# Retention ahead of two expert layers: one PE tiling for three steps, decayed keys on three engines, three load buffers

## The chip, the cores and the metric

The program runs on one core of a Trainium2 chip. The metric is the time of one execution on the device in microseconds (us). Before the change it was 1789.78 us, the median of three runs (1785.21, 1789.78 and 1790.85). Differences under about 0.3% can't be told from no change.

## The reference, cut to what matters

Retention over 4 batches, 8 heads, 576 positions and 64 features gives 2304 rows of 512 values; they pass a mixture of 8 experts whose gate is normalised eight times over rows and columns, and then a two-layer net. Inputs and output are float32.

```python
scores = scale * np.matmul(q, k.transpose(0, 1, 3, 2))
Dmat = np.where(rel >= 0, gamma[:, None, None] ** rel[None, :, :], 0.0)
ret = scores * Dmat[None, :, :, :]
attn_out = np.matmul(ret, v)
# x = attn_out as (2304, 512)
for e in range(8):
    h = np.maximum(x @ w1[e], 0.0)
    out += P[:, e:e + 1] * (h @ w2[e])
# moe2
h = x @ w_in; g = np.maximum(0.01 * h, h); y = g @ w_out
```

## The kernel before

The expert layers take some 1700 us and the change touches none of their code. It lies in the first part, the retention, which is done in 18 chunks (n = 0 to 17; N = 18) of 128 rows. The two halves of the batch alternate, so that even and odd n are two independent streams; each pair works through a sequence of 576 positions in four chunks of 128, and the last two chunks hold the 64-row ends of the sequences. A chunk whose place in its sequence is 0 (n = 0, 1, 8, 9) has no state from earlier chunks.

Each chunk has two loads of 512 KB: `qk` (queries and keys, features on the partitions) and `vk` (values and keys, positions on the partitions). Both come from SyncE's queue (SP), each kind into four rotating buffers. A load into a buffer waits until all readers of the chunk that was there are done. SP also carries the decay tables `gq_t` (256 KB), two halves of the first expert's weights `raw` (1 MB each, at n = 3 and n = 11), the stores of finished operand tiles `x` (256 KB a chunk, from n = 9 on), rows of scales (`s_dram`, `inv`) and the loads of operand tiles back into `xring` (384 KB each).

For chunk n TensorE (PE) does, in this order in pass n of the loop:

- `emit_qk(n + 1)`, L695: scores of the next chunk into two PSUM banks `sc`; VectorE (DVE) multiplies them by the decay mask into `w` (L697)
- `emit_state(n)`, L725: decayed queries `qd` times the running state, into the two banks `xo`
- `emit_du(n)`, L754: decayed keys times values, added to the state's bank `du`; ScalarE (ACT) copies it to `state` (L756)
- `emit_scale(n - 1)`, L764: column sums of the magnitudes `ab` of the chunk before, by a product with ones; DVE makes a power of two of them (L767) and scales both `xo` banks with it into an operand tile (L770)
- `emit_intra(n)`, L735: `w` times values, added to `xo`; ACT takes the magnitudes into `ab` (L739)

The queries are decayed on GpSimd (POOL) two chunks ahead (`decay_q`, L669, 128x512, two buffers `qd`). The keys are decayed one chunk ahead (`decay_k`, L678): three heads (128x192) on DVE and five (128x320) on POOL. A scaled tile is split in a high and a low half: ACT casts (L829), DVE subtracts (L831).

Beside this the first expert's weights are prepared. Their small tasks wait in a list `pre`, and `step()`, called four times a chunk, emits at most one that is ready; `PACE` is the least number of steps between two tasks of the same engine (POOL "G" and DVE "D"). The instructions of an engine run strictly in the order in which they were emitted.

At the end two 512-column products `mark` (L952) start the banks `s2` of the expert layers, and then the first expert product (hA, L1053) begins. The last chunk's `emit_scale` and what hangs on it stand in `drain`, from which `tick` takes one entry when its counter `wait[0]` has run out.

Of the kernel before, what the change touches and what calls it, by code (L numbers as in the profile page):

```python
# [22 lines left out]
NP = H // 2  # L23
# [108 lines left out]
def retention_moe_ffn_kernel(ctx: ExitStack, tc: tile.TileContext, qk, vk, wg, wm, wf,  # L132
# [475 lines left out]
    with ExitStack() as actx:  # L608
# [23 lines left out]
        def load_qk(n):  # L632
            if n < N:
                qks[n] = ain.tile([P, 2, 512], F32, tag="qk", name=f"qk{n}", bufs=4)
                nc.sync.dma_start(qks[n].rearrange("p a x -> p (a x)"), qk[n])

        def load_vk(n):
            if n < N:
                vks[n] = ain.tile([P, 2, 512], F32, tag="vk", name=f"vk{n}", bufs=4)
                nc.sync.dma_start(vks[n].rearrange("p a x -> p (a x)"), vk[n])  # L640
# [9 lines left out]
        for i in range(36):  # L650
            nc.tensor.matmul(wu[:, :P], ones_b, ones_b, start=True, stop=True)
# [3 lines left out]
        nc.vector.memset(low_e, -896.0 * 2.0 ** 23)  # L655
        load_qk(0)
# [5 lines left out]
        load_qk(2)  # L662
        nc.scalar.activation(warm_a, tiny, AF.Abs)
        wt, qds, xo_t, halves, rows_, abs_t = {}, {}, {}, {}, {}, {}
# [6 lines left out]
        def decay_k(n):  # L671

            if n < N - 2:
                kd = vks[n][:, 1].rearrange("p (h d) -> p h d", h=H)
                c = chunk_of(n)[1]
                for e, h, k in ((nc.vector, 0, 3 if n > 1 else H), (nc.gpsimd, 3, H if n > 1 else 3)):
                    if k > h:
                        e.tensor_tensor(kd[:, h:k], kd[:, h:k],  # L678
                                        gk_t[:, c, h:k].unsqueeze(2).to_broadcast([P, k - h, D]), op=ALU.mult)
# [5 lines left out]
        def emit_qk(n):  # L685
# [5 lines left out]
            wt[n] = awk.tile([P, 2, NP, C], F32, tag="w", name=f"w{n}")  # L691
            if n < N - 2:
                for m in range(NP):
# [5 lines left out]
            for pb in range(2):  # L699
                nc.gpsimd.memset(wt[n][rows(pb), :, :, rows(1 - pb)], 0.0)  # L700
            for m in range(NP):
                for pb in range(2):
                    for j in range(2):
                        nc.tensor.matmul(sc[j][rows(pb), m, rows(pb)], kv[rows(j), m, rows(pb)],
                                         qv[rows(j), m, rows(pb)], start=True, stop=True)
            for j in range(2):
# [51 lines left out]
        def emit_scale(n):  # L758
# [4 lines left out]
            for m in range(NP):  # L763
                nc.tensor.matmul(l1, ones_b, ab[:, m], start=(m == 0), stop=m == NP - 1, skip_group_check=True)  # L764
# [88 lines left out]
        PACE = {"G": 2, "D": 3}  # L853
        emit_qk(0)
        for n in range(N):
            load_qk(n + 3)
            load_vk(n + 2)
            keeps(n)
# [13 lines left out]
            def step():  # L872
                wait[0] += 1
                order.t = 0.86 * wait[0]
                if n < 4:
                    return
# [17 lines left out]
                if n >= N - 4:  # L894
                    try_loads()

            decay_q(n + 2)
            if n:
                emit_qk(n + 1)
            step()  # L900
# [5 lines left out]
            if n >= 1:  # L906
                emit_scale(n - 1)
            step()
# [4 lines left out]
            decay_k(n + 1)  # L913
# [9 lines left out]
            step()  # L923
            if n % 2 and 2 * NT_S <= (n - 2) // 2 < 8:
# [13 lines left out]
        wait[0] = 0  # L938
# [10 lines left out]
    s2 = [bank(f"du{i}", f"s2_{i}") for i in range(2)]  # L949
    s1 = [bank(f"x{i}", f"s1{t}") for i, t in enumerate("ab")]  # L950
    def mark(t):
        nc.tensor.matmul(t.rearrange("p (a i) -> p a i", a=4), ones_b,  # L952
                         ones_b.unsqueeze(1).to_broadcast([P, 4, P]), start=True, stop=True)

    for t in s2:
        mark(t)
# [653 lines left out]
```

## Time and profile before

| | |
|---|---|
| median of three runs | 1789.78 us |
| the profiled execution | 1784.0 us |
| its span | 1781.9 us |
| PE busy | 1750.5 us, 98% of the span |
| DVE, ACT, POOL busy | 1500.0, 1262.0 and 821.7 us |
| granted TensorE clock, mean | 0.998 |
| first product of the expert layers | starts at 76.95 us |

The profiled execution is one of its own; the 2.1 us between it and its span lie before the first and after the last instruction. The chain of waits says which work ended last, step by step; "idle before" in a row is the engine's idle time ahead of the instruction, with what ended it. PEld are the weight loads of PE, which run ahead of its products.

### The profile page before, as it was taken

Reading aid. Unit: us, or ns where it says so; the run is one execution under the profiler, and the core shown is the slowest. Engines: PE = TensorE matmul, PEld = TensorE weight load, DVE = VectorE, ACT = ScalarE, POOL = GpSimd, SP = SyncE. Lnnn points to the kernel's source line nnn. Section 1 sums busy time; section 2 is a strip of 40 time slices with the busy share of each in tenths; the row PEclk is TensorE's granted clock in tenths of the full one; section 3 lists DMA queues with packets and bytes.
Section 4 is the critical chain, followed back from the end, with each engine's and each line's share of the span. In section 5 each row is a group of like instructions: output and inputs, shape, how many; then the busy total and the mean of one; then the engine's idle time right before and its main releaser. Section 6 shows DMA issues by size and latency. Waiting matters only on the chain.

```text
span 1781.9 us, 36082 instructions
## 1 busy us (share of the span) xinstructions
PE 1750.5 (98%) x13782; PEld 1275.9 (72%) x13782; DVE 1500.0 (84%) x2660; ACT 1262.0 (71%) x2757; POOL 821.7 (46%) x794
## 2 busy tenths in 40 slices
PE   8999999999999999999999999999999989999998
PEld 7755677777777777777777777777776556777776
DVE  7877899988888888888888888988776887788876
ACT  4667677777777777777777777777675667877653
POOL 3676262635445272625354453636124973444600
PEclk9999999999999999999999999999999999999999
DMA  9854353534544435445354454453443444435232
GB/s 352 312 199 157 116 171 109 191 120 163 158 139 158 159 123 172 144 144 187 113 178 136 146 170 145 138 166 106 136 154 101 160 157 145 144 98 164 81 121 84
DMA packets 205474, 272.48 MB, mean 153 GB/s; under 512 B 13922, under 2 KB 173044, under 8 KB 200180
## 3 DMA queue, kind: packets, MB, share of 16 engines
q1 hardware_dynamic: 205300, 270.17, 46.4%
q8 instruction: 108, 1.77, 0.4%
q14 instruction: 66, 0.54, 0.1%
HBM read 239.31 MB, written 30.81 MB: 152 GB/s over the span
## 4 chain that ended last, share of the span: by engine, by line
PE 92%; DVE 3%; POOL 2%; DMA 1%; issue 1%; ACT 1%; SPq 0%; DVEq 0%; POOLq 0%; ACTq 0%
PE s L1257 17%; PE hA L1084 12%; PE hB L1084 12%; PE hE L1084 12%; PE s1a L1257 12%; PE s1b L1257 11%; PE hD L1084 6%; PE s L1299 2%; PE s1b L1299 1%; PE s1a L1299 1%; PE hE L1053 1%; PE hA L1053 1%; PE hD L1053 1%; PE hB L1053 1%; PE sc L695 1%
## 5 line engine op out<-in xcount | busy, mean ns | idle before, releaser
L1084 PEld LDWEIGHTS <-w 128*128 128x128 f16 x4788 | 468.9, 98 | 237.7 <-issue 3.5
L1257 PEld LDWEIGHTS <-hs 128*128 128x128 f16 x3888 | 380.6, 98 | 88.0 <-ACT hs L1165 4.9
L1257 PEld LDWEIGHTS <-hp 128*128 128x128 f16 x2916 | 285.3, 98 | 82.7 <-issue 3.6
L275 POOL TENSOR_TENSOR w<-raw,w 128x384 f16<-128x384 f32 x148 | 163.7, 1121 | 311.8 <-ACT w L265 311.2
L1270 DVE SCALAR_TENSOR_TENSOR y<-s,fac,y 128x256 f32<-128x256 f32 (+1 forms) x322 | 197.6, 614 | 95.7 <-PE s L1257 80.4
L282 POOL TENSOR_TENSOR raw<-raw 128x256 f32<-128x256 f32 x296 | 268.8, 908 | 19.8
L1257 PE MATMUL s<-w,hs 128*128 128x256 f16 x1932 | 264.3, 273 | 0.2 <-ACT s L1275 0.2
L1084 PE MATMUL hB<-xring,w 128*128 128x384 f16 x1368 | 260.0, 326 | 1.9 <-ACT hB L1094 1.9
L1084 PE MATMUL hA<-xring,w 128*128 128x384 f16 x1368 | 261.1, 327 | 0.0
L1084 PE MATMUL hE<-xring,w 128*128 128x384 f16 x1368 | 260.7, 327 | 0.0
L1175 DVE TENSOR_TENSOR hs<-fs,hs 128x768 f16<-128x768 f32 (+1 forms) x228 | 238.2, 1050 | 12.1 <-ACT hs L1165 11.4
L300 POOL TENSOR_TENSOR w<-raw,w 128x512 f16<-128x512 f32 x148 | 195.6, 1337 | 96.0 <-ACT w L294 95.9
L459 POOL TENSOR_TENSOR f<-f,e 128x256 f32<-128x256 f32 x64 | 53.4, 835 | 365.2 <-DVE e L451 321.2
L1165 ACT ACTIVATE hs<-fs 128x768 f16<-128x768 f32 (+1 forms) x228 | 187.4, 823 | 47.9 <-DVE fs L1200 40.2
L1165 ACT ACTIVATE hp<-fp 128x384 f16<-128x384 f32 x240 | 160.5, 677 | 12.7 <-DVE fp L1123 11.9
L1270 DVE SCALAR_TENSOR_TENSOR y<-s1a,fac,y 128x256 f32<-128x256 f32 (+1 forms) x161 | 98.8, 614 | 51.2 <-ACT s L1275 26.4
L1257 PE MATMUL s1a<-w,hs 128*128 128x256 f16 x972 | 133.6, 273 | 5.5 <-ACT hs L1165 4.4
L1257 PE MATMUL s1a<-w,hp 128*128 128x256 f16 x972 | 132.8, 273 | 1.6 <-DVE y L1270 1.0
L1257 PE MATMUL s1b<-w,hs 128*128 128x256 f16 x960 | 131.5, 273 | 2.1 <-DVE hs L1175 1.7
L1270 DVE SCALAR_TENSOR_TENSOR y<-s1b,fac,y 128x256 f32<-128x256 f32 (+1 forms) x161 | 98.8, 613 | 40.2 <-ACT s L1275 18.1
L1257 PE MATMUL s1b<-w,hp 128*128 128x256 f16 x960 | 131.1, 273 | 1.5 <-DVE y L1270 1.5
L1257 PE MATMUL s<-w,hp 128*128 128x256 f16 x966 | 131.8, 273 | 0.0
(207 smaller groups left out, 2748.2 us busy)
## 6 DMA issues: line engine op xcount, KB each, us to landing
xring<-x SPq DMA_DIRECT2D x407, 384.0 KB, 3.8
raw<-in_wm SPq DMA_DIRECT2D x32, 1024.0 KB, 6.3
r<-in_wf SPq DMA_DIRECT2D x64, 256.0 KB, 3.0
x<-xst SPq DMA_DIRECT2D x51, 256.0 KB, 2.0
qk<-in_qk SPq DMA_DIRECT2D x18, 512.0 KB, 5.1
vk<-in_vk SPq DMA_DIRECT2D x18, 512.0 KB, 8.2
wf_s<-f SPq DMA_DIRECT2D x32, 256.0 KB, 2.6
raw<-wf_s SPq DMA_DIRECT2D x8, 1024.0 KB, 5.8
```

Source lines behind the costliest of these rows:

```text
L275: nc.gpsimd.tensor_tensor(v[0], v[1], v[2], op=ALU.subtract)
L282: nc.gpsimd.tensor_tensor(o, x, y_, op=ALU.subtract)
L300: nc.gpsimd.tensor_tensor(lo, r, hi, op=ALU.subtract)
L459: nc.gpsimd.tensor_tensor(dst, dst, cur["tx"].bitcast(F32), op=ALU.mult)
L695: nc.tensor.matmul(sc[j][:, m], kv[rows(j), m], qv[rows(j), m], start=True, stop=True)
L1053: nc.tensor.matmul(bank, w[:, a, wi, k, :], x[:, :, c, k, :], start=q == k == i == 0, stop=q == k == 1 and i == 2, skip_group_check=True)
L1084: nc.tensor.matmul(bank, w[:, a, wi, k, :], x[:, :, b, k, :], start=r in (1, 5) and k == q == 0, stop=k == 1 and q == 2, skip_group_check= ...
L1165: nc.scalar.activation(hid[k][:, 0, a:b], src[:, a:b], AF.Relu if moe and relu else AF.Copy)
L1175: nc.vector.tensor_tensor(t[:, 1, a:b], src[:, a:b], t[:, 0, a:b], op=ALU.subtract)
L1257: nc.tensor.matmul(out_, t[:, a, i, ts], w[:, b, wi, 0, :], start=start and k == 0, stop=k == 5, skip_group_check=True)
L1270: nc.vector.scalar_tensor_tensor(out_, bank, f, out_, op0=ALU.mult, op1=ALU.add)
L1299: nc.tensor.matmul(bank, t[:, a, i, ts], w[:, b], start=l == g == q == 0, stop=l == g == 1 and q == 2, skip_group_check=True)
```

## The change

The row and column tiling of the product for magnitudes becomes that of the two products on either side of it (two products of 64 output rows in place of one of 128). Keys are decayed on three engines (one head on DVE, six on POOL, one on ACT) at the head of a pass instead of late in it, ahead of `decay_q` and `emit_qk`. POOL's weight tasks stand at least 5 steps apart instead of 2. There are three buffers of each kind, `qk` is loaded two chunks ahead instead of three, and the last `vk` one pass earlier. The zeroing for the two end chunks and their masks are moved, one `mark` goes to the start and one into pass 16, and the drain starts four ticks later.

```diff
 def load_qk(n):
-        qks[n] = ain.tile([P, 2, 512], F32, tag="qk", name=f"qk{n}", bufs=4)
+        qks[n] = ain.tile([P, 2, 512], F32, tag="qk", name=f"qk{n}", bufs=3)
 def load_vk(n):
-    if n < N:
-        vks[n] = ain.tile([P, 2, 512], F32, tag="vk", name=f"vk{n}", bufs=4)
+    if n < N and n not in vks:
+        vks[n] = ain.tile([P, 2, 512], F32, tag="vk", name=f"vk{n}", bufs=3)
...
-        for i in range(36):
+        for i in range(33):
             nc.tensor.matmul(wu[:, :P], ones_b, ones_b, start=True, stop=True)
...
+        s2 = [None, bank("du1", "s2_1")]
+        mark(s2[1])
         load_qk(0)
...
         load_qk(1)
         load_vk(1)
-        load_qk(2)
...
-                for e, h, k in ((nc.vector, 0, 3 if n > 1 else H), (nc.gpsimd, 3, H if n > 1 else 3)):
-                    if k > h:
-                        e.tensor_tensor(kd[:, h:k], kd[:, h:k],
-                                        gk_t[:, c, h:k].unsqueeze(2).to_broadcast([P, k - h, D]), op=ALU.mult)
+                for e, h, k in ((nc.vector, 0, 1), (nc.gpsimd, 1, H - 1)) if n > 1 else ((nc.vector, 0, H),):
+                    e.tensor_tensor(kd[:, h:k], kd[:, h:k],
+                                    gk_t[:, c, h:k].unsqueeze(2).to_broadcast([P, k - h, D]), op=ALU.mult)
+                for i in range(k, H):
+                    nc.scalar.activation(kd[:, i], kd[:, i], AF.Copy, scale=gk_t[:, c, i:i + 1])
...
             for m in range(NP):
-                nc.tensor.matmul(l1, ones_b, ab[:, m], start=(m == 0), stop=m == NP - 1, skip_group_check=True)
+                for i in range(2):
+                    nc.tensor.matmul(l1[rows(i)], ones_b[:, :64], ab[:, m], start=(m == 0), stop=m == NP - 1,
+                                     skip_group_check=True)
...
-        PACE = {"G": 2, "D": 3}
+        PACE = {"G": 5, "D": 3}
         emit_qk(0)
         for n in range(N):
-            load_qk(n + 3)
+            load_qk(n + 2)
             load_vk(n + 2)
+            if n == N - 4:
+                load_vk(N - 1)
...
+            clear(n + 1)
+            if n:
+                decay_k(n + 1)
             decay_q(n + 2)
             if n:
                 emit_qk(n + 1)
+            if n == N - 3:
+                last_masks(N - 2)
             step()
             emit_state(n)
...
             if n >= 1:
                 emit_scale(n - 1)
+            if n == N - 2:
+                last_masks(N - 1)
             step()
             if n:
                 emit_intra(n)
             else:
                 emit_qk(1)
-            decay_k(n + 1)
+                decay_k(1)
...
+            if n == N - 2:
+                s2[0] = bank("du0", "s2_0")
+                mark(s2[0])
...
-        wait[0] = 0
+        wait[0] = 4
```

`clear` zeroes on POOL the parts of an end chunk's `w` that stay zero, and `last_masks` holds the four mask products of an end chunk; both were inside `emit_qk` before.

On SP, near the end of the retention, the loads of the last two chunks (qk16, vk16, qk17, vk17) stand among stores `x0_1<-xf` and loads `xring` like this before:

```order
L635 DMA qk17_1120<-in_qk 128x1024
L640 DMA vk16_1122<-in_vk 128x1024
L499 DMA x0_1_96<-xf11_1051 128x1024
L776 DMA s_dram_90<-s12_1099 1x128
L524 DMA xring_101<-x0_1_96 128x3x512 x2
L640 DMA vk17_1186<-in_vk 128x1024
```

and like this now:

```order
L635 DMA qk16_1181<-in_qk 128x1024
L640 DMA vk16_1183<-in_vk 128x1024
L640 DMA vk17_1185<-in_vk 128x1024
L499 DMA x0_1_96<-xf11_1107 128x1024
L795 DMA s_dram_90<-s12_1162 1x128
L524 DMA xring_101<-x0_1_96 128x3x512 x2
L635 DMA qk17_1260<-in_qk 128x1024
```

The last `vk` moved ahead of the two `xring` loads, and the last `qk` moved behind them. vk17 takes the buffer of vk14, so it waits for chunk 14's values to have been read, and all that follows on SP waits with it.

On DVE, around chunk 9 (w9 is its mask product, vk8 and vk9 the decayed keys), the rows before are:

```order
L767 TENSOR_SCALAR s6_697<-xo6_0_606 128x128
L770 SCALAR_TENSOR_TENSOR y3_114<-xo6_0_606,s6_697 128x256
L770 SCALAR_TENSOR_TENSOR y3_114<-xo6_1_607,s6_697 128x256
L678 TENSOR_TENSOR vk8_590<-vk8_590,gk_t_136 128x192
L831 TENSOR_TENSOR xring_101<-first1_491,xring_101 128x2x256
L226 TENSOR_REDUCE mt0_715<-mg0_669 32x1
L227 STREAM_TRANSPOSE t32_84<-mt0_715 32x32
L697 TENSOR_TENSOR w9_729<-sc9_0_727,dt_t_135 128x512
```

and now:

```order
L786 TENSOR_SCALAR s6_731<-xo6_0_631 128x128
L789 SCALAR_TENSOR_TENSOR y3_114<-xo6_0_631,s6_731 128x256
L789 SCALAR_TENSOR_TENSOR y3_114<-xo6_1_632,s6_731 128x256
L850 TENSOR_TENSOR xring_101<-first1_510,xring_101 128x2x256
L226 TENSOR_REDUCE mt0_747<-mg0_699 32x1
L227 STREAM_TRANSPOSE t32_84<-mt0_747 32x32
L683 TENSOR_TENSOR vk9_680<-vk9_680,gk_t_136 128x64
L704 TENSOR_TENSOR w9_764<-sc9_0_762,dt_t_135 128x512
```

The decay of vk9, a third as wide, stands directly ahead of chunk 9's masks, where that of vk8 stood behind the scaling of chunk 6.

On POOL, chunks 11 to 14, with the weight tasks L360 between the decays, before:

```order
L678 TENSOR_TENSOR vk11_787<-vk11_787,gk_t_136 128x320
L360 TENSOR_TENSOR w0_0_0_895<-raw0_0_382,w0_0_0_895 128x4x128
L669 TENSOR_TENSOR qd13_923<-qk13_847,gq_t_137 128x512
L360 TENSOR_TENSOR w0_0_0_895<-raw0_0_382,w0_0_0_895 128x4x128
L678 TENSOR_TENSOR vk12_849<-vk12_849,gk_t_136 128x320
L360 TENSOR_TENSOR w0_0_1_938<-raw0_0_382,w0_0_1_938 128x4x128
L669 TENSOR_TENSOR qd14_993<-qk14_915,gq_t_137 128x512
L360 TENSOR_TENSOR w0_0_1_938<-raw0_0_382,w0_0_1_938 128x4x128
L678 TENSOR_TENSOR vk13_917<-vk13_917,gk_t_136 128x320
```

and now:

```order
L675 TENSOR_TENSOR qd12_898<-qk12_889,gq_t_137 128x512
L360 TENSOR_TENSOR w0_0_0_944<-raw0_0_389,w0_0_0_944 128x4x128
L683 TENSOR_TENSOR vk12_891<-vk12_891,gk_t_136 128x384
L675 TENSOR_TENSOR qd13_973<-qk13_962,gq_t_137 128x512
L683 TENSOR_TENSOR vk13_964<-vk13_964,gk_t_136 128x384
L675 TENSOR_TENSOR qd14_1046<-qk14_1036,gq_t_137 128x512
L360 TENSOR_TENSOR w0_0_0_944<-raw0_0_389,w0_0_0_944 128x4x128
L683 TENSOR_TENSOR vk14_1038<-vk14_1038,gk_t_136 128x384
```

Four weight tasks that stood within two chunks now stand one in every one or two chunks, and the decay of the keys comes ahead of that of the queries in each pass.

## Rows read from the trace of the kernel before

**Rows 1.** The page's first line.

```profile
span 1781.9 us, 36082 instructions
```

**Rows 2.** Chain of waits, from 55 to 78 us: start us, us, what.

```profile
66.99 0.65 SPq L524
...
69.01 5.91 DMA vk<-in_vk
```

**Rows 3.** Timeline of PE, one chunk: start us, us, engine, line, operation, count.

```profile
35.18 1.16 PE L695 MATMUL sc<-qk 64*128 64x128 f32 x16
36.27 0.67 PE L725 MATMUL xo<-qd,state 64*64 64x128 f32 x16
36.87 0.69 PE L754 MATMUL du<-vk 128*64 128x64 f32 x16
37.48 0.40 PE L764 MATMUL xo<-ab,ones_b 128*128 128x128 bf16 x4
37.81 1.09 PE L735 MATMUL xo<-w,vk 128*64 128x128 f32 x16
38.83 0.60 PE L695 MATMUL sc<-qk 64*128 64x128 f32 x6
```

**Rows 4.** Timeline of PEld at chunks 2, 8 and 12, idle before in brackets.

```profile
15.87 0.43 PEld L725 LDWEIGHTS xo<-qd,state 64*64 64x64 f32 x16 [0.34 <-POOL qd L669]
...
17.90 0.42 PEld L754 LDWEIGHTS du<-vk 128*64 128x64 f32 x10 [1.12 <-POOL vk L678]
...
42.15 0.30 PEld L695 LDWEIGHTS sc<-qk 64*128 64x128 f32 x2 [0.42 <-DVE w L697]
...
60.38 0.42 PEld L754 LDWEIGHTS du<-vk 128*64 128x64 f32 x10 [1.12 <-POOL vk L678]
60.87 0.23 PEld L764 LDWEIGHTS <-ones_b 128*128 128x128 bf16 x4
...
62.22 0.96 PEld L695 LDWEIGHTS sc<-qk 64*128 64x128 f32 x15 [0.17 <-DVE y L770]
```

**Rows 5.** Timeline of DVE, 38 to 47 us.

```profile
39.20 0.35 DVE L678 TENSOR_TENSOR vk<-vk,gk_t 128x192 f32<-128x192 f32 x1
39.46 1.76 DVE L831 TENSOR_TENSOR xring<-first,xring 128x512 f16<-128x512 f32 x1
...
41.46 1.23 DVE L697 TENSOR_TENSOR w<-sc,dt_t 128x512 f32<-128x512 f32 x2
...
43.86 0.69 DVE L831 TENSOR_TENSOR xf<-y,xf 128x512 f16<-128x512 f32 x1
```

**Rows 6.** Timeline of POOL, 38 to 62 us.

```profile
37.85 0.73 POOL L678 TENSOR_TENSOR vk<-vk,gk_t 128x320 f32<-128x320 f32 x1
39.35 1.32 POOL L669 TENSOR_TENSOR qd<-qk,gq_t 128x512 f32<-128x512 f32 x1 [0.78 <-DMA qk<-in_qk]
...
59.15 1.17 POOL L678 TENSOR_TENSOR vk<-vk,gk_t 128x320 f32<-128x320 f32 x1
```

**Rows 7.** Stretches: us, then busy of PE, PEld, DVE, ACT, POOL, clock, DMA, GB/s.

```profile
5.00:35.00 30.00, 26.44 (x459) 21.98 (x458) 23.56 (x54) 12.56 (x32) 11.95 (x12) 1.00 1.03 404
35.00:50.00 15.00, 14.56 (x248) 11.88 (x243) 14.72 (x38) 11.12 (x30) 7.06 (x7) 1.00 0.70 233
50.00:65.00 15.00, 14.02 (x260) 11.51 (x260) 14.29 (x28) 10.22 (x26) 11.73 (x11) 1.00 1.03 396
```

**Rows 8.** The first load of the program (tile qk, 0 to 1 us).

```profile
DMA to landing us min/median/max: 3.5/3.5/3.5
```

**Rows 9.** Timelines of PE and DVE, the end of the retention, 68 to 78 us.

```profile
69.21 1.07 PE L704 MATMUL sc<-qk 64*64 64x64 f32 x30
...
70.38 1.73 DVE L708 TENSOR_TENSOR w<-sc,dt_t 64x256 f32<-64x256 f32 x4 [0.26 <-PE sc L704]
...
75.05 1.09 PE L735 MATMUL xo<-w,vk 128*64 128x128 f32 x16 [0.65 <-DMA vk<-in_vk]
...
76.95 0.65 PE L1053 MATMUL hA<-xring,w 128*128 128x384 f16 x3
```

More of the change, by code (lines that the diff above doesn't have):

```diff
@@ L655, in retention_moe_ffn_kernel, with mark @@
         nc.vector.memset(low_e, -896.0 * 2.0 ** 23)
+        def mark(t):
+            nc.tensor.matmul(t.rearrange("p (a i) -> p a i", a=4), ones_b,
+                             ones_b.unsqueeze(1).to_broadcast([P, 4, P]), start=True, stop=True)
+        s2 = [None, bank("du1", "s2_1")]
+        mark(s2[1])
         load_qk(0)
@@ L661, in retention_moe_ffn_kernel @@
         load_vk(1)
-        load_qk(2)
         nc.scalar.activation(warm_a, tiny, AF.Abs)
+        scs = []
         wt, qds, xo_t, halves, rows_, abs_t = {}, {}, {}, {}, {}, {}
@@ L690, in emit_qk @@
             sc = [bank(f"sc{j}", f"sc{n}_{j}").rearrange("p (m i) -> p m i", m=NP) for j in range(2)]
-            wt[n] = awk.tile([P, 2, NP, C], F32, tag="w", name=f"w{n}")
             if n < N - 2:
+                wt[n] = awk.tile([P, 2, NP, C], F32, tag="w", name=f"w{n}")
                 for m in range(NP):
@@ L698, in emit_qk @@
                 return
-            for pb in range(2):
-                nc.gpsimd.memset(wt[n][rows(pb), :, :, rows(1 - pb)], 0.0)
+            scs.append(sc)
             for m in range(NP):
@@ L705, in emit_qk, with clear, last_masks @@
                                          qv[rows(j), m, rows(pb)], start=True, stop=True)
+        def clear(n):
+            if N - 2 <= n < N:
+                wt[n] = awk.tile([P, 2, NP, C], F32, tag="w", name=f"w{n}")
+                for pb in range(2):
+                    nc.gpsimd.memset(wt[n][rows(pb), :, :, rows(1 - pb)], 0.0)
+        def last_masks(n):
+            if not N - 2 <= n < N:
+                return
+            sc = scs.pop(0)
             for j in range(2):
@@ L874, in step @@
                 order.t = 0.86 * wait[0]
+                if n >= N - 4:
+                    try_loads()
                 if n < 4:
@@ L893, in step @@
                         break
-                if n >= N - 4:
-                    try_loads()
+            clear(n + 1)
+            if n:
+                decay_k(n + 1)
             decay_q(n + 2)
@@ L948, in retention_moe_ffn_kernel @@
     hA, hB, hE, hD = (bank(t, n) for t, n in (("sc0", "hA"), ("sc1", "hB"), ("x0", "hE"), ("x1", "hD")))
-    s2 = [bank(f"du{i}", f"s2_{i}") for i in range(2)]
     s1 = [bank(f"x{i}", f"s1{t}") for i, t in enumerate("ab")]
[L951 to L956, printed above, removed]
     cs = const.tile([P, E], F32, name="cs")
```

## The prediction

> **What bounds the kernel now.** I read the page first: a span of 1781.9 us [rows 1], on the profiled execution's own 1784.0 us, with PE busy for 98% of it. Then the timeline of PE over the first 80 us, since only the retention changes. A chunk there is five groups of products with no gap that counts: scores start at 35.18, state at 36.27, key update at 36.87, magnitudes at 37.48, values at 37.81, the next scores at 38.83 [rows 3]. So a chunk costs 3.65 us and PE sets it. The chunks that cost more show who made PE wait: in chunk 2 PEld stood 0.34 us for the decayed queries and 1.12 for POOL's decay of the keys, in chunk 12 1.12 for the same decay, and at 42.15 it stood 0.42 for DVE's masks [rows 4]. Third, the stretches of the DMA: from 5 to 35 and from 50 to 65 us the sixteen engines are busy all the time (1.03 and 1.03) at about 0.40 MB per us [rows 7]. Nothing more goes through then, and what lands when is decided by the order of issue. Last, the end: the chain runs through the two reloads of `xring`, issued from 66.99, and the last `vk`, issued at 69.01 and landed 5.91 us later [rows 2]; PE waits for it at 75.05, and the first expert product starts at 76.95 [rows 9]. The program behind that is as before, and PE bounds it, so I take the change of this start as the change of the time.
>
> **The change part by part.** Tn is the start of pass n, that is of the scores of chunk n + 1. Before, T8 = 38.83 [rows 3], T14 = 62.22 [rows 4] and T15 = 62.22 + 3.65 = 65.9. State comes 1.09 us into a pass [rows 3], and in pass 2 at 15.87 after its wait [rows 4], so T2 is about 14.6, and T3 would be 18.2 without the waits.
>
> *Warming products and the first mark.* Three products fewer and one 512-column product more at the start; they lie under the wait for the first `qk`, which lands 3.5 us after its issue [rows 8]. Nothing, within 0.3 us either way.
>
> *Keys before queries on POOL.* In chunk 2 POOL did two decays of queries (1.32 [rows 6]) ahead of the keys of that chunk. Now it does one. The keys are ready 1.32 us earlier, less the longer decay: six heads for five, 0.73 x 6/5 = 0.88. So 0.34 + 1.12 = 1.46 of waiting goes, some 1.4 of it for good. What is late next is qk4: with all that is issued ahead of it it is 5.8 MB, at 0.40 MB per us and 2 to 4 us of start and gaps near 17 to 18.5 us, where scores 4 would start at 18.2. I take 1.35 gained; bounds 0.5 and 1.5.
>
> *Three buffers.* A `vk` can now be issued only when PE has read the values of the chunk three back, that is at the start of pass n for chunk n + 2. On an idle DMA it lands 3.5 us later [rows 8], just when pass n + 1 starts and three engines stand ready for it. Where other bytes are ahead it is late. The first `raw` (1.05 MB, 2.6 us) stands ahead of qk6: 9.3 MB are due with it, 23 us and 2 to 4 more as above, so it lands at 25 to 27, against scores 6 at 14.6 + 3 x 3.65 = 25.6 or a little later. I take 0.35 lost (0 to 1). The second `raw` is issued in pass 11 ahead of qk14: vk13, a store, `raw` and qk14 are 2.36 MB, 5.85 us, plus 0.1 to the issue and 2.2 of start and landing (3.5 [rows 8] less 1.3 for that load's own bytes): qk14 lands 8.15 us after T11, where two chunks take 7.3. That is 0.85 lost, and 0.2 more for qk15 behind a store and a table. Bounds 0 and 2.5 for both.
>
> *Wait behind a late vk.* `decay_k` now stands on DVE ahead of the masks, so these, the scaling and the split queue behind the landing. On DVE from masks to the split, 41.46 to 43.86, are 2.40 us, and the split takes 0.69 [rows 5]: 3.1 a chunk, less 0.15 or so for two heads fewer (0.35 for three [rows 5]). There is about 0.6 us of slack in 3.65, and I take no loss, as the masks of a chunk are due one chunk later.
>
> *Spaced weight tasks.* In chunk 12 the decay of keys started at 59.15 behind a weight task and took 1.17 where 0.73 is usual [rows 6]; PEld waited 1.12 [rows 4] and the chunk took 1.3 more than 3.66. With one weight task in 5 steps POOL has 0.88 + 1.32 + 1.3 = 3.5 at most in a chunk of 3.65, and the keys are a chunk ahead. I take the whole 1.3 as gained (bounds 0.6 and 1.3).
>
> *Chunks 8 to 10.* There is no state product (0.6 us) in 8 and 9. So passes 8 to 13 would take 2 x 3.05 + 4 x 3.65 = 20.7; they took 62.22 - 38.83 = 23.39, 2.7 more, of which 1.3 are chunk 12's above and 1.4 lie here. The cause: the split started at 39.46 took 1.76 instead of 0.69, as POOL's decays ran beside it from 39.35 on [rows 5, 6]. POOL's two decays are still there, but one DVE operation fewer meets them. I take half, 0.7 gained (0 to 1.4).
>
> *One tiling for magnitudes.* Before: four products from 37.48 to 37.81, 0.33 us. Now eight of 64 output rows. The nearest row is the value product in the same tiling: 16 in 1.02 us, 0.064 each [rows 3], one after the other, some 0.055 without the change of tiling ahead of them (an estimate: 0.1 to 0.17 for a change, as PEld's gap of 0.17 ahead of scores shows [rows 4]). So eight are 0.44, against 0.33 and a second change of some 0.07, a loss of 0.04. If the two halves run beside each other it is 0.22, a gain of 0.18. I take a gain of 0.05, nearer to the row, times 12 chunks that PE sets: 0.6 (bounds 2.2 gained, 0.5 lost).
>
> The Trainium skill (TensorEngine Tiling (Array Packing), "Key Properties") says that a change of tiling mode drains the engine, and under "Restrictions" that column tiling does without the fast weight load. In the trace the four full-width loads for the magnitudes take 0.23 us together [rows 4]; without the fast path each half would cost as much as a whole one, and by an estimate from this page the eight loads would take 0.46 and the step lose instead of gain. That is the third rival below.
>
> *Moved zeroing and masks, later drain.* The zeroing (2.2 us on POOL) and four mask products leave the path in chunk 15, 0.2 us. The drain's entries are 2 us later, with 13 us of slack to their first reader. Nothing.
>
> *The end.* vk17 no longer waits on the reloads, but qk17 does, and PE needs it earlier: scores 17 open pass 16. SP gets to it only after vk17 has been let go at T15 (chunk 14's values read); behind vk17 come a store, a row and two reloads, 1.35 + 1.3 us of issue. In front of qk17 are then 0.52 + 0.26 + 0.79 MB. By bytes alone, with its own 0.52, qk17 lands 0.1 + 2.2 + 2.09/0.40 = 7.5 us after T15. By the row before, the load behind the two reloads landed 69.01 + 5.91 - 66.99 = 7.93 after the first was issued, which would be 9.3 after T15. I take 8.5. PE would be ready at T15 + 3.3. From qk17 on: scores 0.7, state 0.65, magnitudes 0.3, values 1.0, then the masks of chunk 17 on DVE (1.7 [rows 9], behind the scaling of chunk 15, which ends 2.8 after qk17) until 4.5, and the last values 1.1: 5.6 us to the first expert product, without the two marks that stood before it. Together 14.1 after T15; before it was 76.95 - 65.9 = 11.05. So 3.0 lost (bounds 1.5 and 4).
>
> **The sum.** -1.35 + 0.35 + 1.05 - 1.3 - 0.7 - 0.6 + 3.0 = +0.45, and 0.2 less for the zeroing: +0.25, on 1784.0 of the profiled execution. The runs' median is 1789.78, 5.8 above it; the difference carries over, 1790.0. I round to 1789.8.
>
> **The rivals.**
> First, *the gains stand*: qk17 comes in time, for instance because the reloads are let go later or DMA has room, and `raw` delays nobody. For it: between 35 and 50 us DMA is busy for only 0.70 [rows 7], so it has room there. Against it: from 50 us on it is full. Then -1.4 - 1.3 - 1.0 for the stalls, -0.65 for the last values' wait [rows 9], -0.6 for the marks and -1.5 for the tiling: -6.5, 1783.3.
> Second, slower: *DVE queues behind the keys*. If a late vk lets POOL start first, DVE's own head waits a whole POOL operation, and then once more for the decay of queries (1.32 [rows 6], free after the state product, 1.7 us into a chunk). The masks then end 4.5 us into the chunk, 0.8 after the scores that need their bank. Some 0.6 a chunk over 12 chunks is +7.2, on top of the sum with the end partly hidden under it: +6, 1795.8. It decides as soon as vk lands more than about 0.7 us into the pass. Against it: an idle DMA lands it just at the pass's start.
> Third, *the weights of the halves load slowly*: 0.46 for 0.23 us of loads, +0.17 a chunk instead of -0.05, 12 chunks: +2.6 on the sum, 1792.6.
> Fourth, the change doesn't do what it says: SP is a chunk behind anyway for the rows of scales, so three buffers hold nothing back and neither do the loads arrive otherwise; only POOL's and PE's part is left, 1.4 + 1.3 + 0.6 gained: 1786.5.
>
> **How the numbers follow.** Forecast 0.50, first rival 0.18, second 0.14, third 0.08, fourth 0.10. What a measurement can't tell from no change is 0.3%, 5.4 us. The forecast, the third and the fourth rival lie within it (0.68); of the first some two thirds lie beyond it on the fast side (0.12), of the second some 0.6 on the slow side (0.085). For the spread of the runs (1785.21 to 1790.85) I move 0.04 from the middle to the fast and 0.035 to the slow side: faster 0.16, slower 0.12, same 0.72. The range that holds eight in ten goes from the first rival, a little under it, to the second: 1782.5 to 1795.5; the likeliest case alone is 1786.8 to 1793.8.
>
> **What would show it.** PE waits at scores 17 for DMA `qk`, 4 to 6 us, and not at the last values: that is the end's step. If that wait is under 1 us, the first rival. No wait of PEld on POOL's `vk` in chunks 2 and 12. Short waits of scores 6 and 14 on `qk`. The five starts of a chunk, 3.6 apart with the magnitudes at 0.35 to 0.45: the tiling. Gaps of PEld on the masks in most chunks would mean the second rival. I would be wrong altogether if the chunks between 15 and 65 us took clearly more than 3.66 each, or if the expert layers changed.

## The result and the profile after

The changed kernel takes 1798.86 us (median of five runs, 1796.54 to 1804.38) against 1789.78: ratio 1.0072, 95% interval 1.0057 to 1.0087, slower by 10 to 16 us. (The medians alone lie 9.1 us apart; all ratios here and below are given with their intervals.) The forecast was 1789.8, its range ended at 1795.5. The profiled execution took 1804.38 us:

```profile
span 1802.5 us, 36272 instructions
```

That span is 20.6 us longer than that of [rows 1], of which 13.9 lie ahead of the first expert product (90.81 for 76.95). It belongs to the slowest of the five runs, and the execution traced before (1784.0) was faster than every timed one, so this pair of traces shows more than the timed loss. The waits of PE in the first 250 us (what waited and for whom, us in total, times, longest) show what the trace of before did not have: 9.7 us for loads of `qk` at L702 (before: one wait of 1.1), 6.9 us for the last `qk` at L710, and 2.7 us for `mrow`, the maximum of the gate's values, which DVE finds from a product of PE and PE needs for a later one.

```profile
PE sc L702 <- DMA qk<-in_qk: 9.7, 5, 4.0
PE sc L710 <- DMA qk<-in_qk: 6.9, 1, 6.9
PE s1a L1323 <- DVE mrow L996: 2.7, 1, 2.7
...
PE sc L702 <- DVE w L704: 0.8, 1, 0.8
```

PE's timeline answers to [rows 3] with a chunk that waits for nothing, 37.26 to 40.66, and to [rows 9] with the end:

```profile
31.38 2.08 PE L702 MATMUL sc<-qk 64*128 64x128 f32 x16 [4.04 <-DMA qk<-in_qk]
...
37.26 1.16 PE L702 MATMUL sc<-qk 64*128 64x128 f32 x16
38.35 0.67 PE L742 MATMUL xo<-qd,state 64*64 64x128 f32 x16
38.95 0.69 PE L771 MATMUL du<-vk 128*64 128x64 f32 x16
39.47 0.39 PE L782 MATMUL xo<-ab,ones_b 128*64 128x128 bf16 x8
39.69 1.05 PE L752 MATMUL xo<-w,vk 128*64 128x128 f32 x16
40.66 0.60 PE L702 MATMUL sc<-qk 64*128 64x128 f32 x6
...
66.14 1.16 PE L702 MATMUL sc<-qk 64*128 64x128 f32 x16 [3.43 <-DMA qk<-in_qk]
...
74.54 0.69 PE L710 MATMUL sc<-qk 64*64 64x64 f32 x32
...
84.42 1.14 PE L710 MATMUL sc<-qk 64*64 64x64 f32 x29 [6.87 <-DMA qk<-in_qk]
...
90.81 1.48 PE L1077 MATMUL hA<-xring,w 128*128 128x384 f16 x8
```

The chunk costs 3.40 us instead of 3.65, from magnitudes that start 0.22 us ahead of the values instead of 0.33, from 0.52 instead of 0.61 between update and magnitudes, and from 0.97 instead of 1.02 between values and the next scores. Against that stand the waits at scores 6 (31.38), 14 (66.14) and 17 (84.42). Why qk6 (the `qk` of chunk 6) comes late is on SP's queue (start us, us taken by the issue, what):

```profile
15.64 0.36 SPq L635 DMA_DIRECT2D qk<-in_qk  x1
19.46 0.33 SPq L640 DMA_DIRECT2D vk<-in_vk  x1
19.84 1.40 SPq L645 DMA_DIRECT2D gq_t<-in_c_gq  x1
21.29 0.43 SPq L191 DMA_DIRECT2D raw<-in_wm  x1
...
22.16 0.33 SPq L635 DMA_DIRECT2D qk<-in_qk  x1
...
71.37 3.72 SPq L640 DMA_DIRECT2D vk<-in_vk  x2
...
75.99 2.11 SPq L524 DMA_DIRECT2D xring<-x  x2
78.16 0.60 SPq L635 DMA_DIRECT2D qk<-in_qk  x1
```

From 16.0 to 19.46 SP issues nothing: the next `vk` waits for its buffer. Then come a table, `raw`, and only at 22.16 qk6, which takes 9.08 us (chain of waits):

```profile
22.16 9.08 DMA qk<-in_qk
...
57.27 8.74 DMA qk<-in_qk
```

qk14 is the second row. At the end two `vk` hold SP for 3.72 us, two reloads for 2.11, and qk17 is issued at 78.16. The Trainium skill (DMA: Bandwidth & Descriptors, "Anatomy of one DMA — SWDGE (gpsimd) path") says, of the path by GpSimd, that a wait for a semaphore happens on the issuing sequencer and that the DMA engines only work off their queues. The trace agrees for SP's loads: while SP stood, the engines still worked off what was queued (398 GB/s from 16.0 to 19.5 us), and behind that they ran short (195 GB/s from 19.5 to 22 us). Over 20 to 25 us it is 0.80 and 250 GB/s where [rows 7] has 1.03 and 404 (stretches: busy of PE, PEld, DVE, ACT, POOL, granted clock, DMA, GB/s).

```profile
20.00:25.00 5.00, 5.00 (x104) 4.09 (x102) 4.97 (x9) 2.85 (x7) 3.84 (x4) 1.00 0.80 250
...
30.00:35.00 5.00, 3.62 (x42) 3.10 (x44) 1.51 (x3) 2.81 (x8) 2.42 (x3) 0.50 0.69 270
```

The second row shows the granted clock at 0.50, the lower level of 1.2 GHz: it fell during the wait that ends at 31.38, and the scores behind it take 2.08 us instead of 1.16.

A second trace of the same program (experiment 7) has the waits at scores 14 (3.15 us) and 17 (8.09), but none at scores 6, where qk6 was issued 2 us earlier. So the wait at scores 6 is not there in every execution of the program.

The rest of the loss lies behind the retention. The 97th product of hA, counted in program order, starts at 183.58 us before and at 202.97 after, 106.6 and 112.2 us behind the first. Before:

```profile
183.58 1.14 PE L1084 MATMUL hA<-xring,w 128*128 128x384 f16 x6
```

and after:

```profile
202.97 1.14 PE L1108 MATMUL hA<-xring,w 128*128 128x384 f16 x6
```

So 5.5 us were lost where I had put nothing. The wait for `mrow` is 2.7 of them; the six products behind it ran at a granted clock of 0.52 (163.0 to 166.5 us) and took 2.5 us where the same six take 1.3 in before, and some 1.4 lie ahead of it. In the second trace the clock stayed at 1.00 behind this wait, and 111.2 us lay between the two products. I call 106.6 and 112.2 "the distance" below.

### The profile page after: what moved, and what is told of

It is laid out like the page before. It is cut to its first block, busy times and chain, and to the rows that moved or that the text cites. A ratio compares the mean times of both kernels' runs of the same rounds, so it can differ in the third digit from the quotient of the medians.

```text
span 1802.5 us, 36272 instructions
## 1 busy us (share of the span) xinstructions
PE 1756.3 (97%) x13851; PEld 1280.7 (71%) x13851; DVE 1496.6 (83%) x2662; ACT 1264.2 (70%) x2769; POOL 821.6 (46%) x794
## 4 chain that ended last, share of the span: by engine, by line
PE 87%; DVE 5%; POOL 3%; DMA 3%; issue 2%; ACT 1%; SPq 0%; DVEq 0%; POOLq 0%; ACTq 0%
PE s L1281 17%; PE hA L1108 12%; PE hB L1108 12%; PE hE L1108 12%; PE s1a L1281 12%; PE s1b L1281 11%; PE hD L1108 6%; PE s L1323 2%; DMA qk<-in_qk 1%; PE s1b L1323 1%; PE s1a L1323 1%; DVE xst L577 1%; DMA vk<-in_vk 1%; DVE hs L1199 1%; POOL y L1424 1%
## 5 line engine op out<-in xcount | busy, mean ns | idle before, releaser
L275 POOL TENSOR_TENSOR w<-raw,w 128x384 f16<-128x384 f32 x148 | 163.9, 1123 | 310.7 <-ACT w L265 310.2
```

Of the source, the lines that this page charges most:

```text
L275: nc.gpsimd.tensor_tensor(v[0], v[1], v[2], op=ALU.subtract)
```

## The experiments

Theory A: the loads cost the time. B: the keys' decay at the head of a chunk holds up the engines. C: the later drain disturbs the start of the expert layers. All were timed in five rounds; "before" is the kernel before on the same chip. Starts and distances are each from one traced execution.

**1. The loads taken out of the change, or put alone into the kernel before.**

```diff
-    ... tag="qk", bufs=3)    ... tag="vk", bufs=3)
+    ... tag="qk", bufs=4)    ... tag="vk", bufs=4)
+        load_qk(2)             # ahead of the loop
-            load_qk(n + 2)
+            load_qk(n + 3)
```

> The changed kernel, with four buffers for each of qk and vk again and queries three chunks ahead (the third qk ahead of the loop); everything else of the change stays. Theory A, the loads: the changed kernel lost its time in the waits for qk (4.0 us at scores 6, 3.4 at scores 14, 6.9 at scores 17) and in the half clock that followed each. These waits go, the shorter chunk (3.40 for 3.65 us) stays: first expert product between 67 and 71 us (90.8 changed, 76.95 before), total 1780 to 1785, ratio to before 0.995 to 0.998. Theory B, the keys' decay ahead of the masks holds up the three engines: the first expert product stays above 80 us, total above 1793. Theory C, the later drain disturbs the start of the expert layers: the retention as by A, but 4 to 6 us are lost again between 90 and 170 us, total 1786 to 1790.

Ratio 1.0011 (1.0000 to 1.0022); first product at 76.27, distance 112.0. The loads are worth 0.6%, so A names the largest part, but its figures missed: the first product was due at 67 to 71, and the kernel is no faster than before. Masks (`w`) are now late in three chunks, and PE waits for `mrow` as in the changed kernel.

```profile
PE s1a L1324 <- DVE mrow L997: 2.7, 1, 2.7
PE sc L703 <- DVE w L705: 2.7, 3, 1.4
```

What makes `mrow` late can be read beside before. In both kernels DVE runs `f`, `e` and `hp` ahead of it. Before, POOL stands 1.12 us for ACT's weights, and DVE's three rows run nearly alone:

```profile
144.08 0.29 DVE L432 TENSOR_SCALAR f<-r 128x256 int32<-128x256 int32 x1 [0.19 <-DMA r<-in_wf]
144.28 0.29 DVE L433 TENSOR_SCALAR e<-r 128x256 int32<-128x256 int32 x1
144.49 0.55 DVE L1175 TENSOR_TENSOR hp<-fp,hp 128x384 f16<-128x384 f32 x1
...
144.59 2.09 POOL L275 TENSOR_TENSOR w<-raw,w 128x384 f16<-128x384 f32 x2 [1.12 <-ACT w L265]
```

In the version of this experiment POOL goes on beside them without a pause, and they take 3.50 us for 1.13:

```profile
145.47 1.00 DVE L432 TENSOR_SCALAR f<-r 128x256 int32<-128x256 int32 x1
146.40 1.00 DVE L433 TENSOR_SCALAR e<-r 128x256 int32<-128x256 int32 x1
147.31 1.50 DVE L1200 TENSOR_TENSOR hp<-fp,hp 128x384 f16<-128x384 f32 x1
148.74 0.27 DVE L997 TENSOR_REDUCE mrow<-s1a 1x1 f32<-1x128 f32 x1
...
145.10 2.15 POOL L275 TENSOR_TENSOR w<-raw,w 128x384 f16<-128x384 f32 x2
147.21 2.62 POOL L300 TENSOR_TENSOR w<-raw,w 128x512 f16<-128x512 f32 x2
```

All ten traces with the wait for `mrow` show this, and in the ten without it POOL pauses 1.1 us or more ahead of L275. It is read from traces; no run moved POOL's tasks alone.

The opposite edit in the kernel before (three buffers, two ahead, last `vk` moved up):

> The kernel before with the loads of the change alone: three buffers, queries two chunks ahead, the last vk moved up; old tilings, keys' order, weight tasks and marks. Theory A: waits for qk of 3 to 7 us at scores 6, 14 and 17 appear, granted clock at half behind them, first expert product 88 to 96 us (the changed kernel's 90.8 plus up to 4 for the longer chunk), total 1799 to 1806. Theory B: first expert product below 80 us, total 1789 to 1792. Theory C: as B up to 77 us, nothing behind.

Ratio 1.0054 (1.0040 to 1.0068), first product at 89.07, distance 106.6. The loads alone make the kernel slower, as A says, but nearly all of it sits in one place, scores 17; scores 6 and 14 did not wait.

```profile
81.55 1.15 PE L703 MATMUL sc<-qk 64*64 64x64 f32 x29 [8.52 <-DMA qk<-in_qk]
```

The changed kernel with four buffers, queries still two ahead:

> The changed kernel with four buffers, but queries still two chunks ahead: only the wait of an issue for a free buffer goes. If the buffers hold back the loads: waits for qk under 1 us, first expert product 67 to 72 us, total as with four buffers and three ahead. If the depth does it (qk6 and qk14 are behind raw in the queue whatever the buffers): scores 6 and 14 still wait 1.5 to 4 us and scores 17 for the loads ahead of it, first expert product 74 to 85 us, total 1788 to 1796.

1.0036 (1.0023 to 1.0048), first product at 83.57: depth and buffers each carry a part.

**2. The place of qk17 alone, in the changed kernel.**

```diff
-            if n < N:                       # in load_qk
+            if n < N and n not in qks:
...
             if n == N - 4:
+                load_qk(N - 1)
                 load_vk(N - 1)
```

> The changed kernel with the load of qk17 issued one chunk earlier, ahead of the last vk and of the two reloads of xring. If the order of issue is what makes qk17 late (the step of the prediction on the end): the wait of 6.9 us at scores 17 falls under 2 us, the clock stays up there, first expert product 83 to 87 us for 90.8, total 4 to 7 us under the changed kernel. If the sixteen DMA engines are the bound at that place, the wait moves to the values of chunk 17 and its vk: 88 to 91 us, total the same within 1.5 us.

1.0032 (1.0021 to 1.0044), beside 1.0076 for the changed kernel on the same chip. The wait at scores 17 is gone, the clock is 1.00 from 75 to 85 us, first product at 81.22. The order of issue, not the sixteen engines, made qk17 late. Placing this one load is worth 0.44% of the 0.76%, give or take 0.2.

**3. The tiling alone, in the kernel before.**

```diff
-    nc.tensor.matmul(l1, ones_b, ab[:, m], ...)
+    for i in range(2):
+        nc.tensor.matmul(l1[rows(i)], ones_b[:, :64], ab[:, m], ...)
```

> The kernel before with the magnitudes alone in halves of 64 output rows, the tiling of the update and the values. If the halves run beside each other, as the starts 0.22 us apart in the changed kernel say: 0.25 us less in each chunk that PE sets, first expert product 73 to 75 us, total 2 to 4 us under before, ratio 0.9978 to 0.999. If what shortens the changed kernel's chunk is another engine's relief (fewer weight tasks, keys on three engines): chunks stay at 3.65, ratio 0.9995 to 1.0005. If the loads of the halves cost a whole load each: chunks of 3.8, ratio 1.001.

0.9978 (0.9967 to 0.9990), 3.9 us, 0.25 a chunk, with the starts of the changed kernel:

```profile
32.51 0.69 PE L754 MATMUL du<-vk 128*64 128x64 f32 x16
33.03 0.39 PE L765 MATMUL xo<-ab,ones_b 128*64 128x128 bf16 x8
33.25 1.05 PE L735 MATMUL xo<-w,vk 128*64 128x128 f32 x16
```

Its first product came at 79.14, later than before's 76.95, with chunks 0.25 shorter: a single start scatters (82.78 for the kernel before with the late drain in experiment 4, whose retention is that of before). Only the timed runs decide between small differences.

**4. The late drain.** In the version of experiment 1, and in the kernel before the other way round:

```diff
-        wait[0] = 4
+        wait[0] = 0
```

> The changed kernel with four buffers and queries three ahead, and besides with the drain's first entry four steps earlier, where it stood before (wait 0 for 4). Theory C (the later drain pushes the saturated chain of DVE and POOL behind it, so that the gate's maximum row comes late): PE's wait of 2.7 us for mrow at 148 us and the 4.3 us that the start of the second stage loses go, and the 1.1 us between the first expert product and the 24th with them; ratio to before 0.9975 to 0.999, total 4 to 6 us under the version with the late drain. Rival: the order of drain has no part in it, the chain is late since retention ends otherwise (values of chunk 17, operands kept later): the wait for mrow stays at 2 to 3 us, ratio 1.0005 to 1.0015.

1.0012 (1.0001 to 1.0023): no gain. The wait for `mrow` went, but PE waited 1.5 us for the last chunk's magnitudes (`last_ab`) and 2.3 for ACT's `y` instead; distance 112.5.

> The kernel before with the drain alone later (wait 4 for 0). Theory C: PE waits 2 to 3 us for mrow at about 146 us and the kernel is 4 to 6 us slower than before, ratio 1.0025 to 1.0035. If the late drain hurts only together with the changed end of the retention: ratio 0.9995 to 1.0005, no wait for mrow.

1.0003 (0.9991 to 1.0015), distance 107.1, no wait for `mrow`. C as stated fell: alone, the late drain costs nothing that these runs show.

**5. The keys back behind the values** (four buffers, early drain):

```diff
-            if n:
-                decay_k(n + 1)
             decay_q(n + 2)
...
                 emit_intra(n)
+            decay_k(n + 1)
```

> The same with the early drain, and the keys' decay of each chunk back behind the values of the chunk before (queries first on POOL), still on three engines. Theory B, the masks queue on DVE behind the keys' decay and its landing: PE's waits for w at scores (0.3 to 1.6 us in seven chunks, about 5 us) go, first expert product at 71 to 74 us against 76.3 with the keys at the head, 2 to 4 us less in the total. Against it: POOL's keys are late for the update again in chunks 2 and 12 (1.1 us each) and the time is the same within 1 us, or longer.

1.0008 (0.9996 to 1.0019), distance 112.2. The waits for `w` fell to 0.8 us at the scores, but the time stayed; PE now waited 2.7 us for ACT's part of the keys. What all versions with a distance of 112 shared, against those with 106 to 107, was, among other edits, the spacing of weight tasks. So theory D: the spacing changes the order behind the retention that comes from the planner, the part of the program that books the time of each engine and emits a task when its engine is free. Theory E: the chain of DVE, SP and POOL gives back whatever PE gains.

**6. The spacing.**

```diff
-        PACE = {"G": 5, "D": 3}
+        PACE = {"G": 2, "D": 3}
```

> Four buffers, queries three ahead, early drain, keys behind the values, and now the weight tasks of GpSimd spaced 2 steps again instead of 5; what stays of the change are the magnitudes in halves, the keys on three engines, and the moved masks, zeroing and marks. Theory D: the spacing changes which engine the planner books for the casts of the last operands (the first cast of pair 6 stands on DVE behind it instead of on ACT), so their split, their store on SP and everything that waits for it come late, and PE stands 2 to 4 us for it behind the first expert product. Then the distance from the first hA product to the 97th is 106.6 to 107.5 us as in the kernel before (112.2 with the spacing of 5), and the ratio to before 0.997 to 0.9985. Theory E: that chain is bound by DVE and SP at the end of the retention whatever the spacing, and gives back what PE gains: distance 110 to 113, ratio 0.9995 to 1.001.

0.9978 (0.9967 to 0.9989), distance 108.1: 0.30% for this line.

> The kernel before with the spacing of GpSimd's weight tasks alone, 5 steps for 2. Theory D: distance from the first hA product to the 97th 110 to 113 us instead of 106.6, PE waits 2 to 3 us for the gate, less the 1 us that chunk 12 gains: ratio 1.0015 to 1.0035. Theory E: distance 106.6 to 107.5, ratio 0.999 to 1.0005 (the wait for keys in chunk 12 goes).

1.0017 (1.0006 to 1.0028), distance 112.4. D holds: this line alone lengthens the distance. POOL's last weight task of the retention starts at 70.4 us instead of 57.9, and the first cast of the last operands (`xst`) moves from ACT in the kernel before to DVE in this one:

```profile
69.90 0.62 ACT L69 CAST xst<-y 128x512 f16<-128x512 f32 x1
```

```profile
75.36 0.80 DVE L69 CAST xst<-y 128x512 f16<-128x512 f32 x1
```

The wait of PE here is for ACT:

```profile
143.29 1.43 PE L1016 MATMUL s1a<-wg_s,xring 128*128 128x16 f16 x48 [3.31 <-ACT y L1267]
```

> The changed kernel with the spacing of 2 alone put back. Theory D: the 5.5 us behind the first expert product go, the waits for qk and the half clock stay: first expert product 89 to 92 us, distance to the 97th 106.6 to 108, total 4 to 6 us under the changed kernel, ratio to before 1.004 to 1.005. Theory E: ratio 1.0065 to 1.008.

1.0063 (1.0048 to 1.0078), distance 112.1, `mrow` 2.7: D missed: with the late drain and the late loads still in it, the narrow spacing mends little or nothing (changed kernel: 1.0072 and 1.0076).

> As the first of these, but the keys' decay at the head of a chunk, where the change has it. Theory B (masks queue on DVE behind keys that are still landing): 1 to 4 us slower than with the keys behind the values, waits for w at scores again in several chunks. If the place of the keys is worth nothing once the loads are early: equal within 1 us.

0.9990 (0.9980 to 1.0000), distance 108.7, against 0.9978 with the keys behind, on the same chip: B is right in direction, some 2 us, give or take 2:

```profile
PE sc L703 <- DVE w L705: 5.0, 5, 2.4
```

> The changed kernel with four buffers, queries three ahead and weight tasks 2 steps apart; only the drain stays late (keys at the head). If the late drain is enough by itself to delay the gate in the changed kernel: PE waits 2.7 us for mrow, distance from the first hA product to the 97th 111.5 to 112.5 us, ratio to before 1.000 to 1.002 (0.999 with the early drain). If what the changed kernel with narrow spacing still lost there came from its late loads: distance 107 to 109, ratio 0.9985 to 0.9995.

1.0003 (0.9992 to 1.0013), distance 109.9, and the wait of PE is back:

```profile
PE s1a L1324 <- DVE mrow L997: 2.7, 1, 2.7
```

So in the changed program the wide spacing keeps the distance at 112 with an early drain (experiment 4, where the waits are others), and the late drain brings back the wait for `mrow` with a narrow spacing (2.3 us of time); both had to go. With narrow spacing and early drain, POOL's keys alone were put at the head, and then the drain two steps late (`wait[0] = 2`):

```diff
-            decay_k(n + 1)           # behind the values, all three engines
+            decay_k(n + 1, (1,))     # POOL's six heads, at the head of the pass
...
+            decay_k(n + 1, (0, 2))   # DVE's and ACT's, behind the values
```

> Four buffers, queries three ahead, early drain, weight tasks 2 steps apart, and the keys' decay split in place: GpSimd's part at the head of a chunk, VectorE's and ScalarE's behind the values. If GpSimd gains by keys ahead of queries (no wait of the update for POOL's vk, 1.1 to 2.5 us with the keys late) and VectorE by masks ahead of keys (waits for w, 5 us with the keys first): both sets of waits go, 1 to 3 us under either, ratio to before 0.996 to 0.9975. If GpSimd's operation in progress holds VectorE up wherever the keys stand: as with all keys behind the values, 0.9978 within 0.0005.

0.9990 (0.9980 to 1.0000), distance 107.9: no better than all keys behind.

> The same with the drain's first entry two steps behind the first expert product, between the kernel before (0) and the change (4). If the wait of PE for last_ab (0.9 to 1.5 us at the early drain) can be had without the wait for mrow (2.7 us at the late one): 1 us under the version above. If the chain of DVE, SP and POOL behind it has no slack at all: the wait for mrow comes back in part, 1 to 3 us over it.

1.0014 (1.0005 to 1.0024), distance 113.7: worse than at 0, and the wait for `mrow` is back (2.7). That DVE is slow ahead of `mrow` beside POOL is seen in the rows of experiment 1; why ACT's weights are ready in time for POOL in one order and not in the other stays open.

**7. The lower clock.** Marking products into an idle bank where PE waits, in the changed kernel:

```diff
+            for _ in range({5: 15, 13: 13, 16: 26}.get(n, 0)):
+                mark(s2[1])
             if n:
                 emit_qk(n + 1)
```

> The changed kernel with 15, 13 and 26 more marking products (512 columns each, into the idle bank, some 0.21 us apiece: 3.2, 2.8 and 5.5 us) in front of scores 6, 14 and 17, where PE waits 4.0, 3.4 and 6.9 us for qk. If the half clock after a wait costs time of its own: the granted clock stays at or near 1.00 over the retention, scores after the wait take 1.16 for 2.08 us, the chunks behind the waits 3.4 to 4 for 5.9 and 5.0, first expert product at 84 to 87 us for 90.8, total 4 to 6 us under the changed kernel. If the low clock is only a sign of PE's idleness, and what follows is bound by DVE or loads: first expert product 90 to 92 us, total within 1 us of the changed kernel's.

1.0061 (1.0043 to 1.0079), first product at 86.12. This could not be told from the changed kernel, so both ran once more on one chip:

> The changed kernel as it is, timed beside the others on one chip: ratio to before 1.0055 to 1.008. Its trace is a second execution of the same program: if the waits for qk (4.0, 3.4, 6.9 us) and the 5.5 us behind the first expert product belong to the program they are there again within 1 us; what differs is the scatter of one execution.

> The changed kernel with the marking products in front of scores 6, 14 and 17 once more, beside the changed kernel on one chip. If the half clock behind the waits costs time of its own, as the shorter chunks of the first trace of it say: 3 to 5 us under the changed kernel, ratio of the two 0.997 to 0.9985. If the first trace was a lucky execution: within 1 us.

1.0076 (1.0058 to 1.0094) and 1.0074 (1.0059 to 1.0089): the same, to some 3 us. The trace of the changed kernel missed part of what was expected of it: scores 6 did not wait, and the first product came at 87.70. The changed kernel again, its stretch ahead of scores 17 and the wait:

```profile
75.00:80.00 5.00, 0.00 (x0) 0.00 (x0) 0.00 (x0) 0.08 (x1) 0.00 (x0) 0.73 0.96 274
```

```profile
81.31 1.15 PE L710 MATMUL sc<-qk 64*64 64x64 f32 x29 [8.09 <-DMA qk<-in_qk]
```

and with the marks:

```profile
75.00:80.00 5.00, 4.86 (x23) 1.99 (x21) 0.41 (x2) 0.76 (x4) 0.00 (x0) 1.00 1.00 318
```

```profile
81.39 0.76 PE L710 MATMUL sc<-qk 64*64 64x64 f32 x29 [1.53 <-DMA qk<-in_qk]
```

The clock stayed at 1.00, and from scores 14 to scores 16 PE took 7.16 us (63.88 to 71.04) instead of 9.71 (60.65 to 70.36). But scores 17 began at the same time in both traces: there the landing of qk17 is the bound.

**The sum, measured one edit at a time** (0.1% is 1.8 us):

| from the kernel before, add | ratio | us of the step |
|---|---|---|
| tiling | 0.9978 | -3.9 |
| keys on three engines, masks, zeroing, marks and the call for reloads moved, last `vk` up | 0.9978 | 0 |
| keys at the head | 0.9990 | +2.1 |
| spacing 5 | 1.0012 | +3.9 |
| late drain | 1.0011 | -0.2 (+2.3 with spacing 2) |
| queries two ahead | 1.0036 | +4.5 |
| three buffers: the changed kernel | 1.0072, 1.0076 | +6.4 to +7.1 |

Each ratio has about 0.0012 on either side, so a step is known to some 3 us, and its size depends on the order in which the edits are added (the drain is the case). The best versions are the first two lines, 0.22% under before; beyond the tiling no edit gained anything that could be measured. The call for reloads (`try_loads`) moved from the end of a step to its head in the change, which the list of the change does not name; no run takes it alone.

## Why the prediction was wrong

Two steps failed by size and one by sign. The terms of the loads (1.4 for three buffers and 3.0 for the end) came to 10.9 to 11.6 us in the table, and the spacing cost 3.9 where I had 1.3 gained. Both signs that I had named for being wrong altogether came: from T2 to T13 a chunk took 4.6 us (4.2 in the second trace, 3.9 before), and the expert layers changed.

**Three buffers: the step that failed first.** I took 1.4 us for both `raw` loads, because I let bytes run without a pause at 0.40 MB per us. Scores 6 and 14 waited 4.0 and 3.4 us (none and 3.15 in the second trace): the loads were not issued. SP stood at the `vk` of a buffer that PE had not let go, everything behind it stood too, and the engines ran short (195 GB/s from 19.5 to 22 us, 224 from 50 to 55). qk6 was issued at 22.16 and landed at 31.24; I had 25 to 27. qk14 was issued 2.3 us into pass 11 (57.27 - 54.94), where I had 0.1, and landed 11.1 us into it where I had 8.15. In the kernel before with these loads alone (experiment 2) neither of the two waited, so they need other edits of the change beside the buffers; which ones is not shown.

**The end: the mechanism was right, its size was not.** The wait stands at scores 17, behind vk17's release and two reloads. I had qk17 at T15 + 8.5; it came at 84.42 - 74.54 = 9.9, in the second trace 11.0 (81.31 - 70.36). From T15 to the first expert product it took 16.3 and 17.3 us, not 14.1. With the slower products behind it the term is 5.2 to 6.3 instead of 3.0, against the 11.05 of the one trace of before; the two others with before's loads and tiling (late drain, wide spacing) have 13.2 and 12.8. By time, moving this one load was worth 0.44%, some 8 us.

**Spaced weight tasks: wrong in sign.** PEld no longer waits for POOL in chunk 12 (60.93; [rows 4] had 1.12), as I said, nor in chunk 2 (17.50), where the order of keys and queries did it.

```profile
17.50 0.55 PEld L771 LDWEIGHTS du<-vk 128*64 128x64 f32 x16 [0.17 <-ACT vk L686]
17.97 0.29 PEld L782 LDWEIGHTS <-ones_b 128*64 128x64 bf16 x8
...
60.93 0.55 PEld L771 LDWEIGHTS du<-vk 128*64 128x64 f32 x16 [0.17 <-ACT xf L848]
```

But I counted only the stalls that went. The spacing also shifts when the weight tasks are emitted, and with them the order that the planner gives DVE, ACT and SP behind the retention; instead of gaining 1.3 the line alone cost 3.0 us in the kernel before (1.1 to 5.0), 3.9 in the table. The 0.7 in chunks 8 to 10 did not come either: from T8 to T11 it was 10.9 us (44.07 to 54.94; 10.6 in the second trace) for 11.1 before, less than the tiling's 0.75.

**Moved zeroing and masks, later drain.** "Nothing" was right for the drain in the kernel before (1.0003) and beside the wide spacing (-0.2 us), and wrong beside the narrow one (+2.3). I found 13 us of slack to its first reader, and looked no further than that reader; further on, PE waited 2.7 us for `mrow`.

**Wait behind a late vk.** No loss taken; keys at the head cost 2.1, measured with four buffers, so not behind a load as late as with three. The second rival named this mechanism, and its total (1795.8) was the nearest of mine, but by luck: it priced keys at 6 us, and in the changed kernel PE's gaps on the masks were a small part (0.8 us at the scores).

**One tiling.** Right in sign, 0.6 for a measured 3.9 (1.8 to 5.9): I chose a value near the serial row of [rows 3], and the halves run beside each other. The third rival fell: by the Trainium skill (TensorEngine Tiling (Array Packing), "Restrictions") the halves do without the fast weight load, but eight loads take 0.29 us (17.97) against 0.23 for the four whole ones in [rows 4]; by the rival's estimate, each half at the cost of a whole one, it would be 0.46.

**Keys before queries on POOL.** The stall went, but scores 3 then waited 1.0 us for their load; scores 4 started at 19.22 for 19.75, 0.5 gained of 1.35 (0.2 in the second trace).

The first rival's gains were real only in the tiling; the fourth fell. The range failed on its slow side since I gave the load terms the bounds of a DMA that is always fed, and the expert layers none. (The sum gave 1790.0 and I wrote 1789.8; that changes nothing.)

## What to carry to other kernels

On a strictly ordered issue queue, price a buffer taken away by the time the queue stands, not by bytes: list what stands behind each load that must wait for a release, and put the load that is needed first ahead of the one that must wait. Where a planner orders the work, a change of its table is a change of everything it orders later; compare the order past the edited stage, and follow each chain to the engine that has no slack. One trace is one execution: the first product of the same program came at 90.81 and at 87.70, and with the same retention at 76.95 and 82.78.

## What the runs showed of the hardware

In the changed kernel the granted clock fell to its lower level at the long waits for `qk` (0.50 from 30 to 35 us, scores 2.08 us for 1.16), yet keeping it at 1.00 with products without use gained nothing that could be measured (1.0074 for 1.0076): the next landing was the bound. Where no landing followed, behind the wait for `mrow`, it fell in one trace and not in the other, and the distances were 112.2 and 111.2. Three instructions of DVE took 3.50 us beside POOL's and 1.13 without them (experiment 1). Two products in the two column halves ran beside each other: eight in 0.22 us, where four whole ones took 0.33.
